# Another cut of the last rows of the output projection's weights, and four PSUM banks for the result

## The chip, the cores and the metric

The kernel runs on one core of one Trainium2 chip. The metric is the device time of one execution in microseconds (us), the median over several executions.

The profiles name the engines: PE (TensorE) multiplies, and PEld is its loading of weights; DVE (VectorE) and ACT (ScalarE) copy the result out of PSUM (`ps_s` in the views; the kernel begins each part of the result there at a multiple of 512 columns, and these places are called banks below); SP (SyncE) issues the loads and the first store, ACT the second. A DMA packet is one piece that one of the 16 DMA engines moves, here one contiguous run of bytes on one partition.

## The reference

Grouped-query attention over a cache, for a few new tokens: 32 sequences of 4 tokens, 32 query heads on 4 key/value heads of 128, 2048 cached positions, model width 1024, all in bf16.

```python
q = (x @ wq).reshape(B, Sq, Hq, Dh).transpose(0, 2, 1, 3)
k = jnp.repeat(k_cache, rep, axis=1)
v = jnp.repeat(v_cache, rep, axis=1)
scores = jnp.einsum("bhqd,bhkd->bhqk", q, k) * (Dh ** -0.5)
o = jnp.einsum("bhqk,bhkd->bhqd", _softmax(scores, axis=-1), v)
return o.transpose(0, 2, 1, 3).reshape(B, Sq, Hq * Dh) @ wo
```

Only the last product, with wo (4096 x 1024), is touched by the change.

## The kernel before

All loads go out on one queue in a fixed order: x, wq, the caches of all sequences, then wo. A "row" of wo below is one of 32 blocks of 128 x 1024, one for each step of the accumulation: on a partition it is 1024 columns, 2048 B. Most of wo comes in pieces of four rows; the last two rows come by halves, so that the first 512 columns of the result y can be finished, copied and stored while the other half still arrives.

```python
WO = (4, 4, 4, 4, 4, 4, 2, 2, 1, 1)
NA = 512
NB = 800
COLS = ((0, 0, NA), (512, NA, NB), (1024, NB, D))   # place in PSUM, first column, end
...
pieces = [(sum(WO[:c]), m, 0, D) for c, m in enumerate(WO)] + [(Hq - 2, 1, 0, NA), (Hq - 1, 1, 0, NA), (Hq - 2, 1, NA, D), (Hq - 1, 1, NA, D)]
...
for u in range(Hq - 2):              # one row: one weight load, one matmul per entry of COLS
    oproj(u, (0, 1, 2))
for js in ((0,), (1, 2)):
    for u in (Hq - 2, Hq - 1):
        oproj(u, js)
...
for j, eng in enumerate(("dve", "act", "dve")):
    copy(eng, *COLS[j], j)           # PSUM -> y_sb, fp32 -> bf16
for j, (n0, n1, waits) in enumerate(((0, NA, (0,)), (NA, D, (1, 2)))):
    p.dma(("sp", "act")[j], lambda e, n0=n0, n1=n1: e.dma_start(out_flat[:, n0:n1], y_sb[:, n0:n1]),
          [("oe", i) for i in waits], ("out", j), f"s_o{j}")
```

## Time and profile before

| | before |
|---|---|
| median of 6 runs | 362.09 us (362.04 to 362.9) |
| DMA | 151.66 MB at 420 GB/s, engines full in all slices but the first and the last |
| PE busy | 307.6 us, 85% |
| landing of wo rows 20 to 23 (slowest DMA engine) | 352.80 |
| landing of the last wo piece | 358.02 |
| end of the last matmul, end of the last copy | 358.46, 358.89 |
| second store issued, landed | 358.98, 360.74 |

A landing is the time at which the last of a transfer's 16 completion updates arrives, in the trace's own account of semaphore updates; the views of the profile give it only rounded. The end of this kernel is read from the last four lines of the table: everything earlier is the stream of loads, and nothing in the change makes that stream shorter.

### The profile page before, as it was taken

Reading aid. Unit: us, or ns where it says so; the run is one execution under the profiler, and the core shown is the slowest. Engines: PE = TensorE matmul, PEld = TensorE weight load, DVE = VectorE, ACT = ScalarE, POOL = GpSimd, SP = SyncE. Lnnn points to the kernel's source line nnn. Section 1 sums busy time; section 2 is a strip of 40 time slices with the busy share of each in tenths; the row PEclk is TensorE's granted clock in tenths of the full one; section 3 lists DMA queues with packets and bytes.
Section 4 is the critical chain, followed back from the end, with each engine's and each line's share of the span. In section 5 each row is a group of like instructions: output and inputs, shape, how many; then the busy total and the mean of one; then the engine's idle time right before and its main releaser. Section 6 shows DMA issues by size and latency. Waiting matters only on the chain. (4 is left out here: it accounts for less than half of the span.)

```text
span 360.8 us, 6251 instructions
## 1 busy us (share of the span) xinstructions
PE 307.6 (85%) x3034; PEld 147.0 (41%) x2340; DVE 269.5 (75%) x171; ACT 102.8 (28%) x110; POOL 165.9 (46%) x262
## 2 busy tenths in 40 slices
PE   1988788999999999988999888888888898889896
PEld 1002000445444554444444444443333444448721
DVE  0018799999899888879999888888888888865601
ACT  1014222333333333333333333323222233333100
POOL 8002055255555555554455444455555554444100
DMA  8999999999999999999999999999999999999996
GB/s 323 432 434 431 421 429 432 429 417 432 428 423 425 432 431 427 424 432 431 423 427 432 430 423 429 431 432 423 429 431 432 423 429 431 429 425 431 413 417 243
DMA packets 12251, 151.66 MB, mean 420 GB/s; under 512 B 1360, under 2 KB 2128, under 8 KB 2768
## 3 DMA queue, kind: packets, MB, share of 16 engines
q1 hardware_dynamic: 12096, 151.39, 99.1%
q8 instruction: 6, 0.10, 0.1%
q10 hardware_dynamic: 144, 0.13, 0.1%
q14 instruction: 5, 0.04, 0.0%
HBM read 151.26 MB, written 0.26 MB: 420 GB/s over the span
## 5 line engine op out<-in xcount | busy, mean ns | idle before, releaser
L328 DVE STREAM_TRANSPOSE KT_sb<-big 128x2048 f32<-128x2048 f32 x64 | 146.6, 2293 | 16.3 <-DMA big<-in_k_cache_dram 16.3
L354 ACT ACTIVATE P_sb<-ps_s,negmx 128x2048 bf16<-128x2048 f32 x32 | 82.2, 2569 | 184.7 <-DVE negmx L350 184.7
L16 PE MATMUL ps_s<-KT_sb,QD_sb 128*128 128x512 bf16 x384 | 103.7, 377 | 0.0
L385 POOL COPY PD_sb<-PT_sb 32x1024 f32<-32x1024 f32 x62 | 64.3, 1036 | 63.1 <-PE ps_r L394 60.2
L385 POOL COPY big<-PT_sb 32x1024 f32<-32x1024 f32 x61 | 63.2, 1036 | 58.6 <-PE ps_r L394 55.8
L350 DVE TENSOR_REDUCE negmx<-ps_s 128x1 f32<-128x2048 f32 x32 | 73.2, 2287 | 12.4 <-PE ps_s L16 10.8
L394 PE MATMUL ps_r<-big 128*128 128x128 bf16 x1024 | 59.8, 219 | 11.6 <-PEq L85 11.6
L394 PE MATMUL ps_r<-big,PD_sb 128*128 128x128 bf16 x1024 | 59.8, 219 | 9.9 <-PEq L85 9.8
L394 PEld LDWEIGHTS ps_r<-big 128*128 128x128 bf16 x1024 | 57.9, 98 | 22.3 <-issue 21.9
L394 PEld LDWEIGHTS ps_r<-big,PD_sb 128*128 128x128 bf16 x1024 | 58.0, 98 | 21.1 <-issue 20.6
L341 PE MATMUL ps_s<-KT_sb,QD_sb 128*128 128x512 bf16 x128 | 48.3, 377 | 18.1 <-PEq L85 18.1
L341 PEld LDWEIGHTS ps_s<-KT_sb,QD_sb 128*128 128x128 bf16 x128 | 12.3, 96 | 102.8 <-issue 102.8
L363 DVE STREAM_TRANSPOSE PT_sb<-P_sb 128x1024 f32<-128x1024 f32 x32 | 39.8, 1245 | 16.0 <-ACT P_sb L354 16.0
L318 POOL COPY QD_sb<-QT_sb 32x64 f32<-32x64 f32 x128 | 29.6, 231 | 46.1 <-DVE QT_sb L297 20.5
L16 PE MATMUL ps_r<-ident 128*128 128x384 bf16 x173 | 33.3, 325 | 0.0
L366 PEld LDWEIGHTS ps_r<-ssum,permf 128*128 128x128 f32 x64 | 11.9, 187 | 24.8 <-issue 23.1
L403 ACT ACTIVATE QT_sb<-ps_r,rinv 128x128 bf16<-128x128 f32 x32 | 11.8, 368 | 29.6 <-PE ps_r L394 27.3
L279 DVE TENSOR_SCALAR KT_sb<-ps_r 128x512 bf16<-128x512 f32 x2 | 1.3, 688 | 20.1 <-PE ps_r L263 20.1
L420 PE MATMUL ps_s<-big,KT_sb 128*128 128x512 bf16 (+1 forms) x34 | 12.5, 375 | 1.9 <-DMA big<-in_wo_dram 1.0
L434 DVE CAST P_sb<-ps_s 128x512 bf16<-128x512 f32 (+1 forms) x2 | 1.1, 542 | 15.2 <-PE ps_s L420 15.2
L16 PE MATMUL ps_s<-big,KT_sb 128*128 128x224 bf16 (+1 forms) x62 | 12.0, 272 | 0.0
L252 PE MATMUL ps_r<-ident 128*128 128x384 bf16 x32 | 10.3, 322 | 0.0
(41 smaller groups left out, 85.8 us busy)
## 6 DMA issues: line engine op xcount, KB each, us to landing
big<-in_k_cache_dram SPq DMA_DIRECT2D x32, 2048.0 KB, 18.5
big<-in_v_cache_dram SPq DMA_DIRECT2D x32, 2048.0 KB, 22.1
big<-in_wq_dram SPq DMA_DIRECT2D x4, 2048.0 KB, 14.0
big<-in_wo_dram SPq DMA_DIRECT2D x6, 1024.0 KB, 22.9
big<-in_wo_dram SPq DMA_DIRECT2D x2, 512.0 KB, 24.4
big<-in_wo_dram SPq DMA_DIRECT2D x2, 256.0 KB, 22.6
big<-in_wo_dram SPq DMA_DIRECT2D x4, 128.0 KB, 17.5
P_sb<-in_x_dram SPq DMA_DIRECT2D x1, 256.0 KB, 2.7
```

What stands on the lines that cost most here:

```text
L16: return eng.add_instruction(mybir.InstMatmult(name=nc.get_next_instruction_name(), engine=eng.engine, start_tensor_calc=start, stop_tenso ...
L318: p.op("pool", lambda e, s=src, d=dst: e.tensor_copy(d, s), waits if g == 0 else [("pt", i - 2)] * (g == 1 and i > 1), ("qd", i) if g == G ...
L328: p.op("dve", lambda e, s=src, d=dst: e.transpose(d, s), waits, ("kt", i, c), gives="t_kt" if c else None)
L341: mm = lambda e, a_=(out_, lhsT, rhs), f=first, l=last: e.matmul(a_[0], lhsT=a_[1], rhs=a_[2], start=f, stop=l, skip_group_check=True)
L350: p.op("dve", lambda e: e.tensor_reduce(negmx[:, i % 4:i % 4 + 1], ps_s[:, :], AX.X, ALU.max, negate=True), [("qk", i)], ("negmx", i))
L354: p.op("act", lambda e: e.activation(P_sb[:, :, :, :].rearrange("p t r w -> p t w r"), ps_s[:, :].rearrange("p (t w r) -> p t w r", w=2, r=R),
L363: p.op("dve", lambda e: e.transpose(dst, src), [("exp", i)], ("pt", i))
L366: p.op("pe", lambda e: e.matmul(ring[(i if i == L else i // 2 * 2) % 4][:, 510 + i % 2:511 + i % 2], lhsT=permf[:, :], rhs=ssum[:, i % 4:i ...
L385: p.op("dve" if i >= B - 2 and g < i - B + 4 else "pool", lambda e, s=src, d=dst: e.tensor_copy(d, s), [free] * (g == 0 or i >= B - 2) + [ ...
L394: p.op("pe", lambda e: e.matmul(buf[:, 0:Dh], lhsT=pd_of(i)[:, t // 2, :, :, :, t % 2].rearrange("p x g q -> p (x g q)"), rhs=big[:, slot_ ...
L403: p.op("act", lambda e: e.activation(dst, src, ACT.Copy, scale=rinv[:, i % 4:i % 4 + 1]), [("pv", i), ("rinv", i)], ("o", i))
L420: mm = lambda e, a=(out_, lhsT, rhs): e.matmul(a[0], lhsT=a[1], rhs=a[2], start=(u == 0), stop=(u == Hq - 1), skip_group_check=True)
```

## The change

Four rows, not two, are cut; they are cut at column 768, not 512; and y lies in four PSUM banks, so that each of the two stores is fed by one copy on DVE and one on ACT, each with a bank of its own. The intent is that after the last bytes have arrived there are only 256 columns left to multiply, copy and store, while four late rows leave the copies of the first 768 columns enough time.

```diff
-    WO = (4, 4, 4, 4, 4, 4, 2, 2, 1, 1)
-    NA = 512
-    NB = 800
-    COLS = ((0, 0, NA), (512, NA, NB), (1024, NB, D))
+    WO = (4, 4, 4, 4, 4, 4, 2, 1, 1)
+    NA = 768
+    LATE = 4
+    NB = NA + 144
+    COLS = ((0, 0, NA // 2), (512, NA // 2, NA), (1024, NA, NB), (1536, NB, D))
...
-        ... + [(Hq - 2, 1, 0, NA), (Hq - 1, 1, 0, NA), (Hq - 2, 1, NA, D), (Hq - 1, 1, NA, D)]
+        ... + [(u, 1, 0, NA) for u in range(Hq - LATE, Hq)] + [(Hq - LATE, LATE - 1, NA, D), (Hq - 1, 1, NA, D)]
...
-            for j, eng in enumerate(("dve", "act", "dve")):
+            for j, eng in enumerate(("dve", "act", "act", "dve")):
...
-            for j, (n0, n1, waits) in enumerate(((0, NA, (0,)), (NA, D, (1, 2)))):
+            for j, (n0, n1, waits) in enumerate(((0, NA, (0, 1)), (NA, D, (2, 3)))):
...
-        for u in range(Hq - 2):
-            oproj(u, (0, 1, 2))
-        for js in ((0,), (1, 2)):
-            for u in (Hq - 2, Hq - 1):
+        for u in range(Hq - LATE):
+            oproj(u, (0, 1, 2, 3))
+        for js in ((0, 1), (2, 3)):
+            for u in range(Hq - LATE, Hq):
                 oproj(u, js)
```

More of the change, by code (lines that the diff above doesn't have):

```diff
@@ L218, in bass_standalone__gqa_block_cached__sampling_kernel @@
         wo_v = wo.rearrange("(h p e) n -> p h (e n)", p=128, e=4)
-        pieces = [(sum(WO[:c]), m, 0, D) for c, m in enumerate(WO)] + [(Hq - 2, 1, 0, NA), (Hq - 1, 1, 0, NA), (Hq - 2, 1, NA, D), (Hq - 1, 1, NA, D)]
-        assert sum(WO) == Hq - 2
+        pieces = [(sum(WO[:c]), m, 0, D) for c, m in enumerate(WO)] + [(u, 1, 0, NA) for u in range(Hq - LATE, Hq)] + [(Hq - LATE, LATE - 1, NA, D), (Hq - 1, 1, NA, D)]
+        assert sum(WO) == Hq - LATE
         for c, (u, m, n0, n1) in enumerate(pieces):
@@ L224, in bass_standalone__gqa_block_cached__sampling_kernel @@
             dst, src = wo_at(u, m), wo_v[:, u // 4, u % 4 * D:(u % 4 + m) * D]
-            if m == 1:
-                dst, src = dst[:, n0:n1], src[:, n0:n1]
+            if n1 - n0 < D:
+                dst, src = [v.rearrange("p (m n) -> p m n", m=m)[:, :, n0:n1] for v in (dst, src)]
             p.dma("sp", lambda e, dst=dst, src=src: e.dma_start(dst, src),
```

## The prediction

> **What bounds the kernel now.** I read the page first: the share of each engine, the chain of work that ended last, and the slices. Shares say that PE is busy for 85% of the span, but the DMA engines are full in every slice except the first and the last, so the kernel runs at the pace of 151 MB arriving at 420 GB/s. The chain agrees: what ended last goes back through the loads of wo.
>
> ```profile
> DMA 8%; PE 2%; SPq 1%; DVE 0%; issue 0%
> DMA  8999999999999999999999999999999999999996
> GB/s 323 432 434 431 421 429 432 429 417 432 428 423 425 432 431 427 424 432 431 423 427 432 430 423 429 431 432 423 429 431 432 423 429 431 429 425 431 413 417 243
> ```
>
> The first line is the chain by engine, the others are the 40 slices. The change leaves everything before the last wo loads alone, so only the last slice can move. There I took stretches of about a microsecond (columns: length, then busy time of PE, weight loads, DVE, ACT, POOL, clock, DMA share, GB/s).
>
> ```profile
> 354.00:355.00 1.00, 1.00 (x9) 0.27 (x3) 0.00 (x0) 0.00 (x0) 0.00 (x0) 1.00 1.02 382
> 355.00:356.00 1.00, 1.00 (x9) 0.22 (x3) 0.00 (x0) 0.00 (x0) 0.00 (x0) 1.00 1.04 360
> 356.00:357.00 1.00, 1.00 (x9) 0.19 (x2) 0.00 (x0) 0.00 (x0) 0.00 (x0) 1.00 0.67 231
> 357.00:358.00 1.00, 1.00 (x7) 0.29 (x3) 0.17 (x1) 0.00 (x0) 0.00 (x0) 1.00 0.18 63
> 358.00:359.00 1.00, 0.46 (x4) 0.10 (x1) 0.89 (x2) 0.41 (x1) 0.00 (x0) 1.00 0.00 0
> 359.00:360.00 1.00, 0.00 (x0) 0.00 (x0) 0.00 (x0) 0.00 (x0) 0.00 (x0) 1.00 0.49 165
> ```
>
> The loads die away between 356 and 358, because the 16 DMA engines do not finish together: in the trace's completion times the first engine ends the last wo piece at 356.29 and the slowest at 358.02, and this lag of 1.7 to 1.9 us is the same for every wo piece. PE is busy without a gap until 358.5, then the copies and the two stores follow. The timeline shows how close PE and the loads are:
>
> ```profile
> 357.10 0.10 PEld L420 LDWEIGHTS ps_s<-big,KT_sb 128*128 128x128 bf16 x1 [0.26 <-DMA big<-in_wo_dram]
> 357.20 0.83 PE L420 MATMUL ps_s<-big,KT_sb 128*128 128x512 bf16 x3
> 357.40 0.10 PEld L420 LDWEIGHTS ps_s<-big,KT_sb 128*128 128x128 bf16 x1 [0.20 <-DMA big<-in_wo_dram]
> 357.73 0.10 PEld L420 LDWEIGHTS ps_s<-big,KT_sb 128*128 128x128 bf16 x1 [0.23 <-DMA big<-in_wo_dram]
> 357.83 1.06 DVE L434 CAST P_sb<-ps_s 128x512 bf16<-128x512 f32 x2 [15.20 <-PE ps_s L420]
> 358.06 0.30 PE L420 MATMUL ps_s<-big,KT_sb 128*128 128x288 bf16 x1
> 358.20 0.26 PE L16 MATMUL ps_s<-big,KT_sb 128*128 128x224 bf16 x1
> 358.40 0.41 ACT L432 ACTIVATE P_sb<-ps_s 128x288 bf16<-128x288 f32 x1 [16.11 <-PE ps_s L420]
> 358.55 0.35 SPq L439 DMA_DIRECT2D out_dram<-P_sb  x1
> 358.98 0.37 ACTq L439 DMA_DIRECT2D out_dram<-P_sb  x1
> ```
>
> The last four weight loads each wait for a wo piece (30 and 31 by half rows), and the last piece lands at 358.02, 0.04 before its matmul at 358.06. So the end of the kernel is: last landing, one pair of matmuls, copy, store. DVE makes both the 512-column and the 224-column copy in one run of 1.06, ending 358.89; the ACT store is issued at 358.98 and lands at 360.74.
>
> [...] The packet records agree: median 312 ns for 8192 B, 162 for 4096, 85 for 2048, 46 for 1024. That is about 9 ns plus 37 ns per 1024 B, so a 1536 B packet is estimated at 64 ns and one of 512 B at 27.5 ns. No packet of 512 B is in this trace. [...] The trace agrees: a row of three matmuls, 1024 columns, repeats every 0.434 to 0.436 us, and 224 columns last 259 ns. [...] the casts here fit it, 692 ns for 512 columns and 392 for 224. ACT copies took 602 ns for 512 columns on average and 412 for 288, so some 168 + 0.85 per column.
>
> **The change, part by part.**
>
> Loads. Before, rows 26 and 27 come together, 28 and 29 alone, then 30 and 31 as 512 columns twice. After, 26 to 27 come alone, 28 to 31 as 768 columns, then one transfer with 256 columns of three rows, then 256 columns of row 31. The bytes are the same, and the last stage has the same 262 KB (4 rows of 256 columns for 2 of 512), so the early 768 columns are complete when the early 512 were, near 357.4. What changes is the number of packets. An engine gets eight partitions of each piece. Before it moved from row 26 on: 8 of 4096, 16 of 2048, 32 of 1024 bytes. After: 16 of 2048, 32 of 1536, 32 of 512. With the medians above before is 8x162 + 16x85 + 32x46 = 4128 ns, after is 16x85 + 32x64.4 + 32x27.5 = 4301, so 0.17 us more, plus one completion write of 9 ns. At the very end the slowest engine ran somewhat faster than the medians (0.33 us per 128 KB piece, 41 ns a packet), once others had stopped. I therefore go piece by piece from row 27 landing near 355.43: 28 at 355.95, 29 at 356.46, then with 60 ns a packet 30 at 356.94 and 31 at 357.42, the three-row piece at 24.5 ns a packet at 358.01, and the last at 358.20. The last landing is 0.18 us later than 358.02. This lies on the path.
>
> PE. All rows up to 27 now have four matmuls, not three: 28 more in all at about 2.5 ns, 0.07 us, most of it beside loads that PE waits for. In the last stage three rows become free at once at 358.01[...], so PE comes to row 31 at about 358.39, later than its landing. Its matmuls end at 358.39 + 0.226 = 358.61 (144 columns) and 358.39 + 0.062 + 0.213 = 358.66 (112 columns). Before these ends were 358.36 and 358.46. On the path this costs 0.2 us.
>
> Copies. The 768 columns are copied as 384 on DVE (0.56) and 384 on ACT (0.49) from about 357.78, done by 358.35, so neither queue holds up the last copies; before, DVE's 224 columns waited from 358.46 to 358.52. The last ones are 144 columns on ACT, 0.29, ending 358.94, and 112 on DVE, 0.27, ending 358.97 with the usual 0.04 after the matmul. Before, DVE ended at 358.89. So 0.08 of the 0.2 is left as a loss; the smaller copies give back 0.12.
>
> Stores. The first store (1536 B per row) can be issued near 358.40, so its packets, 8 per engine at 64 ns from some 0.85 after the issue, are over by 359.8 before those of the second start. The second is issued near 359.06. Before, it landed 1.765 us after its issue, of which 8 packets of 46 ns are data; with 27.5 ns it saves 8 x 18.5 = 0.148, giving 1.617. It lands at 360.68 where it was 360.74.
>
> Sum: +0.18 for the landing, +0.02 more for PE, -0.12 for copies, -0.15 for the store: -0.07 us. On 362.12 that is 362.05.
>
> **Rivals.** First: small packets are dearer than the line through four sizes says. If 512 B took as long as 1024 B, the last stage would need 32 x 18.5 = 0.6 us more, and the store would save nothing: about 362.9. Against it speaks how straight the line is; for it, that no such packet was seen. Second: loads are hidden anyway or the tail speeds up[...], and the last landing stays at 358.0; then copies and store count in full, -0.25, 361.85. For it speaks that the last 1024 B packets went at 41 ns. Third: the queue of SP. Before, the issue of one 128 KB piece was held for 6.29 us and the last was issued only at 346.60[...]. Against it: 7 us of lead[...]. Fourth: PE, which has 12 rows of 0.435 to do from the landing of rows 20 to 23 at 352.80, ends at 358.06 with hardly any slack, and becomes the bound through the fourth matmul: +0.05.
>
> **Range and chances.** The terms are tenths of a microsecond and cancel. Repeats of the kernel before lie at 362.06, 362.12 and 362.90, so a median can wander by 0.2 to 0.3. Rival two sets the low side, rivals one and three the high side: 361.65 to 362.5. Two per cent is 7.2 us, more than the whole tail from the last landing to the end, so a change beyond it needs something that no view shows: 0.01 faster, 0.01 slower.
>
> **What would show it.** Right: the last wo landing 0.1 to 0.25 us later; 512 B packets near 27 ns; matmuls of row 31 back to back with those of row 30; ACT and DVE last copies under 0.3 us each, ending within 0.04 of each other; the second store landing some 1.6 us after its issue. Wrong: a PE idle stretch of over 0.2 us in the last stage (packets or queue), the last SP issue later than 355, a store of 512 B rows as slow as one of 1024 B, or a second store whose packets queue behind the first's.

The sum stands: +0.18, +0.02, -0.12 and -0.15 came to -0.07 us, so 362.05. Cut from the PE term is the time of three rows of 256 columns, which came to 0.335 us and led to 358.39 (in the changed kernel they took 0.346). Cut too are the formulas by which matmuls and casts were reckoned; estimates from the trace of the kernel before give nearly the same. Matmuls of 128 and 224 columns last 219 and 259 ns there, and the line through them gives 226 for 144 and 212 for 112; those of 288 and 224 columns start 123 and 96 ns before the next, which gives 62 for 144; the casts of 692 and 392 ns give 559 for 384 columns and 275 for 112. For the 2.5 ns of a fourth matmul in each row the two traces give 3: in the median rows of 1024 columns repeat every 434 ns with three matmuls and every 437 with four. Of the third rival, what was said of the places in SP's queue and of the cost of a late issue is cut; shown is that the last piece landed 11.4 us after its issue at 346.60.

## The result, and the profile after

The changed kernel takes 362.19 us (median of 6, 362.12 to 362.37) against 362.09 (362.04 to 362.9). The ratio is 0.9999 with a 95% interval of 0.9986 to 1.0012. Ratios here are the mean time of one kernel's runs over that of the other's of the same rounds, so not quite the ratio of the medians quoted; here the one run of 362.9 in the mean of before makes the difference.

The page of the changed kernel: the chain that ended last by engine, and the slices of DMA load.

```profile
DMA 8%; PE 3%; SPq 1%; issue 0%; DVE 0%
DMA  8999999999999999999999999999999999999996
GB/s 323 434 434 430 425 427 430 430 419 425 431 425 427 429 429 429 426 429 430 429 425 430 430 425 429 429 432 421 432 427 434 420 432 429 434 420 430 414 417 242
```

Before the last slice nothing differs by more than 7 GB/s, as it should be. The same stretches as in the prediction, of the changed kernel:

```profile
356.00:357.00 1.00, 1.00 (x10) 0.19 (x2) 0.00 (x0) 0.00 (x0) 0.00 (x0) 1.00 0.73 237
357.00:358.00 1.00, 1.00 (x5) 0.20 (x2) 0.09 (x1) 0.00 (x0) 0.00 (x0) 1.00 0.32 95
358.00:359.00 1.00, 0.65 (x9) 0.37 (x4) 0.74 (x2) 0.78 (x2) 0.00 (x0) 1.00 0.00 0
```

Between 357 and 358 the DMA engines are busy for 0.32 of the time, not 0.18: the loads end later. After 358 there is more PE work, and the copies are shared out evenly (DVE 0.74, ACT 0.78, where it was 0.89 and 0.41). The timeline of the changed kernel's end:

```profile
357.53 0.34 PE L421 MATMUL ps_s<-big,KT_sb 128*128 128x384 bf16 x1
357.71 0.33 PE L16 MATMUL ps_s<-big,KT_sb 128*128 128x384 bf16 x1
357.91 0.56 DVE L435 CAST P_sb<-ps_s 128x384 bf16<-128x384 f32 x1 [15.44 <-PE ps_s L421]
358.06 0.24 PE L421 MATMUL ps_s<-big,KT_sb 128*128 128x144 bf16 x1
358.07 0.89 ACT L433 ACTIVATE P_sb<-ps_s 128x384 bf16<-128x384 f32 x2 [15.94 <-PE ps_s L16]
...
358.40 0.23 PE L421 MATMUL ps_s<-big,KT_sb 128*128 128x144 bf16 x1
358.47 0.21 PE L16 MATMUL ps_s<-big,KT_sb 128*128 128x112 bf16 x1
358.65 0.35 SPq L440 DMA_DIRECT2D out_dram<-P_sb  x1
358.72 0.27 DVE L435 CAST P_sb<-ps_s 128x112 bf16<-128x112 f32 x1 [0.26 <-PE ps_s L16]
359.08 0.37 ACTq L440 DMA_DIRECT2D out_dram<-P_sb  x1
```

The three-row piece lands at 358.01 and the last one at 358.20. PE runs four rows of 256 columns back to back from 358.06 and ends at 358.68, the copies end at 358.99, the second store is issued at 359.08 and lands at 360.77. The first store is issued only at 358.65, which will matter.

### The profile page after: what moved, and what is told of

The parts are those of the page before. It is cut to its first block, busy times and chain, and to the rows that moved or that the text cites. A ratio compares the mean times of both kernels' runs of the same rounds, so it can differ in the third digit from the quotient of the medians.

```text
span 360.8 us, 6288 instructions
## 1 busy us (share of the span) xinstructions
PE 307.0 (85%) x3066; PEld 147.2 (41%) x2342; DVE 269.2 (75%) x171; ACT 103.0 (29%) x111; POOL 165.3 (46%) x262
## 5 line engine op out<-in xcount | busy, mean ns | idle before, releaser
L395 PE MATMUL ps_r<-big 128*128 128x128 bf16 x1024 | 59.8, 219 | 11.4 <-PEq L85 11.4
L16 PE MATMUL ps_s<-big,KT_sb 128*128 128x384 bf16 (+2 forms) x92 | 14.1, 256 | 0.0
L421 PE MATMUL ps_s<-big,KT_sb 128*128 128x384 bf16 (+1 forms) x36 | 11.1, 317 | 2.1 <-DMA big<-in_wo_dram 1.1
L435 DVE CAST P_sb<-ps_s 128x384 bf16<-128x384 f32 (+1 forms) x2 | 0.8, 415 | 15.7 <-PE ps_s L421 15.4
```

The lines of the kernel that those rows point to most:

```text
L16: return eng.add_instruction(mybir.InstMatmult(name=nc.get_next_instruction_name(), engine=eng.engine, start_tensor_calc=start, stop_tenso ...
L395: p.op("pe", lambda e: e.matmul(buf[:, 0:Dh], lhsT=pd_of(i)[:, t // 2, :, :, :, t % 2].rearrange("p x g q -> p (x g q)"), rhs=big[:, slot_ ...
L421: mm = lambda e, a=(out_, lhsT, rhs): e.matmul(a[0], lhsT=a[1], rhs=a[2], start=(u == 0), stop=(u == Hq - 1), skip_group_check=True)
```

## The experiments

The landing of any one piece moves by up to 0.3 us from run to run: the fastest of the 16 DMA engines ends rows 20 to 23 of wo at 350.80 to 351.06 in the fourteen traces of the table below, the slowest between 352.74 and 353.06. To compare traces I therefore count from the landing of rows 20 to 23, which come in the same way, as one piece, in all these kernels, and split the rest into five terms that follow each other: to the last landing, on to the end of PE, to the end of the last copy, to the issue of the second store, to its landing. All in us:

| run | last landing | PE | copy | issue | store | sum | median time |
|---|---|---|---|---|---|---|---|
| before | 5.223 | 0.441 | 0.430 | 0.087 | 1.768 | 7.949 | 362.09 |
| before_again | 5.220 | 0.440 | 0.428 | 0.087 | 1.758 | 7.933 | 362.12 (one run) |
| after | 5.405 | 0.481 | 0.312 | 0.087 | 1.693 | 7.978 | 362.19 |
| a_again | 5.373 | 0.482 | 0.312 | 0.087 | 1.699 | 7.953 | 362.13 |
| e_singles | 5.554 | 0.333 | 0.309 | 0.088 | 1.679 | 7.963 | 362.19 |
| e_store_cut | 5.407 | 0.489 | 0.310 | 0.088 | 1.581 | 7.875 | 362.14 |
| e_copies_only | 5.211 | 0.440 | 0.429 | 0.087 | 1.748 | 7.915 | 362.17 |
| e_loads_only | 5.391 | 0.474 | 0.420 | 0.030 | 1.678 | 7.993 | 362.26 |
| e_whole_rows | 5.204 | 0.659 | 0.596 | 0.030 | 2.070 | 8.559 | 362.84 |
| e_late2 | 5.248 | 0.421 | 0.486 | 0.030 | 1.993 | 8.178 | 362.44 |
| e_late6 | 5.755 | 0.336 | 0.309 | 0.088 | 1.644 | 8.132 | 362.46 |
| v_640_even | 5.223 | 0.386 | 0.393 | 0.088 | 1.780 | 7.870 | 362.00 |
| v_640_act_last | 5.239 | 0.386 | 0.381 | 0.085 | 1.799 | 7.890 | 362.11 |
| v_512_act_last | 5.238 | 0.440 | 0.434 | 0.085 | 1.753 | 7.950 | 362.13 |

The two traces of each of the two kernels lie 0.016 and 0.025 apart in the sum. Differences under about 0.03 are therefore not used. The experiments ran on three chips; the kernel before, run beside them, had medians of 362.22 in the first group (the changed kernel again, singles, store cut, copies only), 362.15 in the second (loads only, whole rows, two and six late rows) and 362.12 in the third.

My theory when I began: the change's shorter copies and second store are real, but are used up by the later last landing, which the greater number of packets causes, and by the second store's packets standing behind those of the first. The rival: a store takes a fixed time from issue to landing, and the rest is chance.

### The changed kernel and the kernel before, again

No edit.

> The changed kernel again, as the anchor for this chip. Both theories: within 0.15 us of the kernel before; in the profile the last wo piece lands near 358.20, the second store is issued near 359.08 and lands near 360.77, 1.69 us after its issue.

> The kernel before, for a second trace. The landing of rows 20 to 23 of wo moves by up to 0.3 us from run to run with the slowest DMA engine, so I measure from there to the landing of the second store: 7.949 in the first trace of this kernel. Expected 7.93 to 7.97, second store 1.75 to 1.78 after its issue; if it scatters by more than 0.05, differences of that size between the other runs say nothing.

The changed kernel: 362.13 against 362.22, ratio 0.9994 (0.9978 to 1.001), last landing 358.21, store issued at 359.09, landed at 360.79 after 1.70. The kernel before, one look: sum 7.933. Both as expected. With the means of two traces each, the change costs +0.167 in the last landing and +0.041 on PE, and gives back 0.117 in the copies and 0.067 in the store: +0.024 together, within the scatter.

### The first store cut short (wrong result)

```diff
-e.dma_start(out_flat[:, n0:n1], y_sb[:, n0:n1])
+e.dma_start(out_flat[:, n0:min(n1, n0 + 256)], y_sb[:, n0:min(n1, n0 + 256)])
```

> The changed kernel, wrong on purpose: the first store writes only its first 256 columns (512 B per row, as the second), 512 columns of the output stay unwritten. My theory: the first store's packets are over before the second's start, so the second lands 1.60 to 1.64 us after its issue, as I predicted for it, against 1.69 in the changed kernel, and the end comes 0.05 to 0.09 earlier. Rival (the time from issue to landing is fixed): 1.69 again and no gain.

The output is wrong (two thirds of the first 768 columns are never written). The DMA view of the last 2 us, 40 slices of 0.05 us, first of the changed kernel:

```profile
DMA  0000000000598979998989899730000000000000
DMA packets 288, 0.26 MB, mean 131 GB/s; under 512 B 32, under 2 KB 288, under 8 KB 288
out_dram<-P_sb ACTq DMA_DIRECT2D x1, 64.0 KB, 1.7
```

then with the first store cut:

```profile
DMA  0000000000001699852002689952000000000000
DMA packets 288, 0.13 MB, mean 66 GB/s; under 512 B 32, under 2 KB 288, under 8 KB 288
out_dram<-P_sb ACTq DMA_DIRECT2D x1, 64.0 KB, 1.6
```

In the changed kernel the two stores are one block: the first one's packets last until 360.20, the second's begin at 360.02. With the first store cut there are two humps with a gap, and the second store, itself unchanged, takes 1.581, 0.115 less than the mean of 1.696 of the two traces of the changed kernel. So the stores do meet, and the rival of a fixed time falls. The packets say the same: from its issue to the end of its last data packet the second store takes 1.224 here and 1.326 in both traces of the changed kernel, so the queue costs about 0.10; the rest, up to the landing, is 0.357 here and 0.367 and 0.373 there. The clock shows only 362.14 (361.94 to 362.16): in this trace the slowest DMA engine came about 0.1 later than in that of the changed kernel, which the sums leave out.

### Whole rows, no cut

```diff
-WO = (4, 4, 4, 4, 4, 4, 2, 1, 1)
+WO = (4, 4, 4, 4, 4, 4, 2, 1, 1, 1, 1, 1, 1)
-        for js in ((0, 1), (2, 3)):
-            for u in range(Hq - LATE, Hq):
-                oproj(u, js)
+        for u in range(Hq - LATE, Hq):
+            oproj(u, (0, 1, 2, 3))
```

(and no pieces beside those of WO)

> The changed kernel with rows 28 to 31 whole, 2048 B packets only, each row multiplied at once in order. My theory (the later landing comes from the number of packets): the last wo piece lands at 357.95 to 358.06, against 358.20; but then all of row 31, four matmuls and all four copies follow the landing, so the second store is issued near 359.5 and lands near 361.2, 0.4 to 0.5 later than the changed kernel. Rival (the landing is set by the bytes): it lands at 358.2 too.

The landing comes 5.204 after rows 20 to 23, where the changed kernel has 5.405 and 5.373. The bytes are the same; 64 packets per DMA engine for rows 28 to 31 have become 32. That is 0.17 to 0.2 us less, as expected from fewer packets. But this run has two transfers fewer as well, so by itself it does not tell packets from transfers; the run with single rows below does. The absolute landing, 358.13, lies 0.07 above the stated window; the slowest engine landed rows 20 to 23 at 352.92 in this run, 0.13 later than in the trace of the changed kernel. And the timeline shows why rows are cut at all:

```profile
358.17 0.10 PEld L421 LDWEIGHTS ps_s<-big,KT_sb 128*128 128x128 bf16 x1 [0.52 <-DMA big<-in_wo_dram]
358.55 0.74 DVE L435 CAST P_sb<-ps_s 128x384 bf16<-128x384 f32 x2 [15.91 <-PE ps_s L421]
358.71 0.67 ACT L433 ACTIVATE P_sb<-ps_s 128x384 bf16<-128x384 f32 x2 [16.41 <-PE ps_s L16]
359.30 0.35 SPq L440 DMA_DIRECT2D out_dram<-P_sb  x1
359.41 0.37 ACTq L440 DMA_DIRECT2D out_dram<-P_sb  x1
```

Everything follows the last landing, both stores are issued 0.12 apart, and the second takes 2.07. Against this run, the cut of the changed kernel is worth 0.6 us in the sum.

### Two late rows

```diff
-LATE = 4
+LATE = 2
-WO = (4, 4, 4, 4, 4, 4, 2, 1, 1)
+WO = (4, 4, 4, 4, 4, 4, 2, 2, 1, 1)
```

> The changed kernel with two late rows, not four. My theory: 32 fewer packets of the smaller sizes per engine than in the changed kernel, so the last landing is back at 358.0 to 358.06, as in the kernel before; but the 768 columns are complete only near 357.66, ACT is still copying its 384 columns until 358.7 and its 144 columns end near 359.0, the second store is issued near 359.1 behind a first store issued at 358.8, and lands near 360.85, 0.08 later than the changed kernel. Rival (the landing alone sets the end): 0.15 earlier than the changed kernel.

The landing is back at that of the kernel before (5.248; before 5.223 and 5.220), yet the sum is 8.178, 0.21 more than that of the changed kernel. The rival that the landing alone sets the end is out. The timeline of this run:

```profile
358.24 0.74 DVE L435 CAST P_sb<-ps_s 128x384 bf16<-128x384 f32 x2 [15.48 <-PE ps_s L421]
358.40 0.67 ACT L433 ACTIVATE P_sb<-ps_s 128x384 bf16<-128x384 f32 x2 [15.98 <-PE ps_s L16]
358.98 0.35 SPq L440 DMA_DIRECT2D out_dram<-P_sb  x1
359.10 0.37 ACTq L440 DMA_DIRECT2D out_dram<-P_sb  x1
```

The loss came where I had expected it, but was larger: the first store was issued at 358.98 (expected 358.8), 0.12 before the second, which then took 1.99. This is what the four late rows of the change are for: with 768 columns in the first store, two rows leave its copies no time.

### The late columns of each row in a transfer of its own

```diff
-[(Hq - LATE, LATE - 1, NA, D), (Hq - 1, 1, NA, D)]
+[(u, 1, NA, D) for u in range(Hq - LATE, Hq)]
```

> The changed kernel with the three-row piece of 256 columns cut into three single rows, two transfers more. My theory (the two stores share a queue of packets): the last wo piece lands at 358.20 to 358.24, PE takes rows 28 to 30 as they land, so the last copy ends near 358.85 and the second store is issued near 358.94, 0.14 earlier than in the changed kernel; but its packets then stand behind those of the first store, issued near 358.65 as before, so it lands 1.73 to 1.80 us after its issue, near 360.70, and only half of the 0.14 is kept. Rival (a store takes the same time from issue to landing whatever else is under way): 1.69 after its issue, 360.63, and all of it is kept.

PE gains what was expected: its term falls from 0.481 to 0.333, since rows 28 to 30 are multiplied as they land. But the last landing is 0.15 to 0.18 later (5.554), where I had expected at most 0.04, and the sum stays at 7.963. My expectation of an earlier issue was wrong, so the run does not test the stores. The packets of both kernels are the same, and so is the time at which they are over: the last data packet of the loads ends 4.928 after the landing of rows 20 to 23 here, 4.955 and 4.922 in the changed kernel (4.781 and 4.732 before, 4.716 with whole rows). What grows is the time from there to the last landing: 0.63 here, 0.45 in both traces of the changed kernel, 0.44 and 0.49 before. So the packets do set the 0.18 by which the change's loads end later, and what the two further transfers cost comes after the last packet, between it and the last completion update. Why is open. The first completion update does not show it: from that of the 768 columns of row 31 to that of the last piece it is 0.847 us here and 0.845 in the changed kernel, while the last update takes 0.872 here and 0.714 there.

### Six late rows, each in transfers of its own

```diff
-LATE = 4
+LATE = 6
-WO = (4, 4, 4, 4, 4, 4, 2, 1, 1)
+WO = (4, 4, 4, 4, 4, 4, 1, 1)
```

(on top of the edit of the last run)

> Six late rows, each in pieces of its own (single rows). My theory: last landing near 358.30, second store issued near 359.02; the first store is issued near 358.25 and its packets are over before the second's start, so the second lands 1.60 to 1.64 after its issue, near 360.64, 0.1 earlier than the kernel before. Rival (fixed store): 1.69 after its issue, 360.71. A few hundredths from each other in the clock, plain in the profile.

The first store was issued at 358.61 (expected 358.25) and its packets are over at 360.13, before the second's first packet at 360.35; the second takes 1.644, at the edge of what was expected without a queue, and less than 1.69. From its issue to its last data packet it takes 1.221, as with the first store cut (1.224); the rest takes 0.42, not 0.36, which no run explains. The landing is 5.755, at least 0.35 later than in the changed kernel, where 0.10 was expected: the same miss as in the last run, with more transfers: the last packet ends at 5.056, 0.12 later than the mean of the changed kernel, as expected, but the landing follows only 0.70 after it. The sum, 8.132, and the clock, 362.46 against 362.15, are worse than before.

### Only the banks and copies of the change

```diff
-    COLS = ((0, 0, NA), (512, NA, NB), (1024, NB, D))
+    COLS = ((0, 0, NA // 2), (512, NA // 2, NA), (1024, NA, NB), (1536, NB, D))
```

(with four copies as in the change, NA = 512, NB = 800 and the loads of before)

> The kernel before with only the banks and copies of the change: 256 and 256 columns copied by DVE and ACT for the first store, 288 and 224 for the second; loads as before. My theory: the last landing stays at 358.02, the second store is issued near 358.97 (before 358.98), since DVE's wait for its own first copy was 0.06 at most; end within 0.05 of the kernel before. The rival that the four banks are what helps and the loads only hurt would have the end 0.1 or more earlier than before.

The copy term is 0.429, as before (0.430, 0.428). The sum is 7.915, 0.026 under the mean of before, most of it a shorter second store (the first is issued at 358.28, well ahead). The banks alone buy nothing that can be told from scatter: DVE's last copy began 0.04 after its matmul in the kernel before too, so it had not been waiting for DVE's first one.

### Only the loads of the change

```diff
-    COLS = ((0, 0, NA // 2), (512, NA // 2, NA), (1024, NA, NB), (1536, NB, D))
+    COLS = ((0, 0, 512), (512, 512, NA), (1024, NA, D))
-            for j, eng in enumerate(("dve", "act", "act", "dve")):
+            for j, eng in enumerate(("dve", "act", "act")):
```

(the second store waits for the third copy alone, and each row is multiplied in three parts)

> The changed kernel's loads with three banks: 512 columns copied by DVE and 256 by ACT for the first store, 256 by ACT alone for the second. My theory: last landing 358.20 as in the changed kernel, the one last copy takes 0.39 in place of 0.29, so the second store is issued near 359.18 (changed kernel 359.08) and lands near 360.86, 0.1 later than the changed kernel. If the last copies do not lie on the path, 360.77.

The one copy of 256 columns takes 0.383 and its term is 0.420 in place of 0.312, as expected. But the store is issued 0.030 after its end and not 0.087 (the last experiment shows why), so the path loses 0.05 and not 0.1; the sum is 7.993 against 7.978 and 7.953. So in the change the split of the last copy over two banks is worth about half of what the shorter copy says.

### Three versions that might beat both

Two late rows of 640 and 384 columns (fewer small packets than the change, a first store earlier than with 768), with the last copies split evenly; the same with ACT finishing last; and 512 columns with ACT finishing last.

```diff
-LATE = 4
+LATE = 2
-WO = (4, 4, 4, 4, 4, 4, 2, 1, 1)
+WO = (4, 4, 4, 4, 4, 4, 2, 2, 1, 1)
-NA = 768
-NB = NA + 144
+NA = 640            # 512 in the third
+NB = NA + 192       # 176 in the second, 240 in the third
-("dve", "act", "act", "dve")
+("dve", "act", "dve", "act")      # second and third only
```

> Two late rows of 640 and 384 columns, four banks, copies 320 and 320, then 192 on ACT and 192 on DVE. My theory (landing by number of packets, then copies, then stores that share the engines): last landing as in the kernel before, 5.2 to 5.25 after rows 20 to 23; second store issued about 0.1 earlier than before relative to them, but only 0.35 after the first, so it takes 1.74 to 1.80 and the whole is 7.83 to 7.88 (before 7.95, copies alone 7.915). Rival (a store's time is its size alone): it takes 1.65 and the whole is 7.75.

> As the last, but DVE copies the first 176 of the last 384 columns and ACT the other 208, so that ACT, which issues the second store, finishes last. In the traces the issue follows the end of ACT's own copy by 0.03 and that of DVE's by 0.088. Expected: issue 0.05 earlier than with the even split, of which the queue behind the first store takes back half or more: 7.80 to 7.86.

> Two late rows of 512 and 512 columns as before, four banks, DVE copies 240 and ACT then 272 of the last half. The first store is issued near 0.6 before the second, so none of its packets are in the way: second store 1.71 to 1.75; issue 0.05 earlier than in the run with copies only. Expected 7.85 to 7.90 from the landing of rows 20 to 23.

The first has the smallest sum of all right kernels, 7.870, 0.07 under the mean of before, and a median of 362.00 (361.97 to 362.12) against 362.12 (362.06 to 362.31). Its ratio is 0.9996 (0.9983 to 1.001): the trace says a gain of 0.07 us, the clock cannot tell it from none. Its end:

```profile
357.91 0.90 DVE L435 CAST P_sb<-ps_s 128x320 bf16<-128x320 f32 x2 [15.38 <-PE ps_s L421]
358.04 0.66 ACT L433 ACTIVATE P_sb<-ps_s 128x320 bf16<-128x320 f32 x2 [15.85 <-PE ps_s L16]
358.58 0.35 SPq L440 DMA_DIRECT2D out_dram<-P_sb  x1
358.89 0.37 ACTq L440 DMA_DIRECT2D out_dram<-P_sb  x1
```

The second store is issued 0.1 earlier than in the kernel before and takes 1.780, not the 1.65 that its size alone would give: again the queue behind the first store, as expected. The other two versions missed what was expected, with sums of 7.890 and 7.950: with ACT finishing last the issue still came 0.085 after the end of its copy, where three other runs (loads only, whole rows, two late rows) show 0.030 after ACT's last copy. My expectation from those was wrong. The instruction records of the traces show what differs. The second store waits for two copies; the copy that its list of waits names first is waited for by the store instruction itself, the other by a separate instruction on ACT just before it, which lasts 17 ns. In the two versions and in the changed kernel the copy that ends last has the separate wait, and the store starts 0.085 to 0.088 after that copy; with two late rows and with whole rows the store itself waits for it, with the loads alone there is no separate wait, and it is 0.030. So the difference goes with the place of the wait and not with the engine of the copy. A version with the waits in the other order was not run.

## Why the prediction was right

Said: 362.05, with 0.98 for a change under 2%. Measured: 362.19, and no difference from before. The number alone proves little, since 2% is longer than all that follows the last landing. By its own steps:

- **Loads.** Right in mechanism, and in size partly by luck. Said: the three-row piece at 358.01, the last at 358.20. Measured: 358.012 and 358.198. Packets of 512 B took 27 ns in the median, but those of 1536 B 67 where 64 was estimated: the prediction's own sum of medians then gives 0.26 more, not 0.17. Row 31's 768 columns landed at 357.48 where 357.42 was said, and the slowest engine needed 0.71 for the last two pieces where 0.78 was said; the two misses cancel. That it is the packets is shown by the runs with whole rows and with single rows together.
- **PE.** Right: ends said 358.61 and 358.66, measured 358.63 and 358.68, without a gap in the last stage (from row to row 0.122, 0.112 and 0.112, 0.346 for the first three rows).
- **Last copies.** Right in the sum: said 0.12 less, measured 0.117 less; 0.29 and 0.27 each. The reading beside it, that DVE's 224 columns had waited until 358.52 in the kernel before, was wrong: the record has them start at 358.50, 0.04 after their matmul, and the run with the copies alone shows that nothing was to be had there.
- **Stores.** This step failed, though only in tenths. Said: the first store issued near 358.40, its packets over by 359.8 before the second's start, the second taking 1.617. Measured: issued at 358.65, packets until 360.20, and 1.693 for the second. The root is mainly in "copied ... from about 357.78": I added for row 31 only the time from the start of one matmul to that of the next, for its 768 columns. The timeline has the second matmul of 384 columns start at 357.71 and last 0.33, so it ended at 358.03 and ACT began to copy at 358.07. In this trace matmuls of 384 columns that follow each other start 0.16 apart, and each lasts 0.33. The difference, 0.16, which I call the drain, I had counted for the last stage, but not for this one. Two smaller misses add to it: these columns landed 0.06 later than said, and the first store's packets took 0.70 from the first to the last, where 8 x 64 ns were counted. The second store with nothing in its way takes 1.581 (first store cut) or 1.644 (six late rows), so the 1.617 was sound for the case that it assumed; standing in the queue cost about 0.10 by the packets, 0.05 to 0.115 by the landings.
- **Sum.** Said -0.07; measured between the means of two traces +0.024. The difference, about 0.09, is the store term (0.067 gained, not 0.148) and two hundredths from PE (0.041 after the landing, not 0.02), less a hundredth from the landing.
- **Rivals.** Packets of 512 B were not dearer than the line. The tail sped up by 0.07 more than was counted, which the dearer 1536 B packets took back. Rival one's own terms add up to 362.8 rather than 362.9, and either lies above the range that it was said to set. SP's issues were held again (that of the last piece from 348.77 for 2.92 us, until 351.69), but 351.69 is well ahead of its landing at 358.20. PE did not become the bound before the last stage (its weight loads waited for wo 7 times, the last until 358.06).

That both kernels measure the same is thus no sign that the change does nothing. Its parts move the end by +0.17, +0.04, -0.12 and -0.07 us, each to be seen in the traces.

## What to carry to other kernels

Cutting the last loads finer shortened what follows the last landing here (2.57 us after it in the changed kernel, 2.73 before, 3.36 with whole rows), but the cuts had their price in packets (estimated at about 9 ns for each packet of one DMA engine, from the medians of 46, 85, 162 and 312 ns for 1024 to 8192 B; 24 packets more per engine moved the last landing by 0.17) and in transfers (two more cost 0.16, after the last packet), so the best cut is found by adding both up; here two late rows at 640 columns come out ahead of both four at 768 and two at 512, by less than the clock can show. When an early store is meant to be out of the way of a late one, follow its own chain to the last packet, with the drain of the matmul that feeds it: a second store that was issued 0.43 us after a first one of 1536 B rows stood behind its packets here, one issued 0.86 us after did not. And where the end depends on the slowest of 16 DMA engines, count from a landing that both kernels share, otherwise its scatter (0.3 us here) hides differences of a tenth.

## Other times from these traces

- Median times of packets: 9 ns for 4 B (16 of them for each transfer, taken for its completion writes), 27 for 512 B, 46 for 1024, 67 for 1536, 85 for 2048, 162 for 4096, 312 for 8192 (after 340 us; those of 512 and 1536 B in the changed kernel, the others in the kernel before).
- From issue to landing, stores of 64 KB with nothing in their way took 1.57 and 1.58 us (first store cut) and 1.64 (six late rows), first stores of 128 KB 1.71 to 1.73, and that of 192 KB in the changed kernel 1.89. A second store of 64 KB issued 0.12 us after a first took 2.07 (whole rows).
- The 16 completion updates of one and the same transfer are far apart: 1.68 to 2.16 us between the first and the last for wo rows 20 to 23 (1.92 in the kernel before, 1.83 in the changed one), and the last of them moves by 0.3 us from run to run.
- In the kernel before, rows of 1024 columns, each with one weight load for three matmuls, repeat every 0.434 to 0.436 us.
- From the end of a copy to the issue of the store that waits for it: 0.030 us where the store itself waits for that copy, 0.085 to 0.088 where a separate instruction before it does.
- More transfers of the same packets moved the last landing after the last packet was over: 0.63 us from packet to landing with 17 transfers of wo, 0.45 with 15.
